# Windowed attention with a gated FFN: tap sums of the second block on TensorE, half swaps by ScalarE copies

## The chip, the cores and the metric

One core of a Trainium2 chip runs the whole program. The metric is the device time of one execution in microseconds (us). TensorE does matrix products, VectorE and ScalarE work elementwise, SyncE issues all DMAs from one queue, and GpSimd does little here.

## The reference

`x` is (4, 4096, 192), `weight_gen` (4, 4096, 8 heads, 7 taps), all fp32.

```python
w = exp(weight_gen - max(weight_gen, -1)); w = w / (sum(w, -1) + 1e-9)   # softmax over 7 taps
out = einsum('bshk,bskhg->bshg', w, x_unf)   # x_unf: tokens s-6 .. s, 8 heads of 24 channels
gate = 1 / (1 + exp(-(out @ w_gate)))        # 192 -> 1536
return (gate * (out @ w_val)) @ w_out        # 1536 -> 192
```

## The kernel before

Channels lie on the partitions and tokens along the free axis. The 16384 tokens are cut into 32 blocks of 512, and the 1536 hidden channels into 12 chunks of 128. A unit is one block with one chunk; there are 384, and `period(s)` gives TensorE the 28 matmuls of one: for unit s the gate and value products (18 matmuls), and for unit s − 2 the output products (10). Two 64-row matmuls run as a pair in the two halves of the array. To keep fp32 accuracy every operand is split in a high and a low part, and each product takes three matmuls (high × high, high × low, low × high).

The inputs of a block are `A` (channels 0 to 127, high and low), `As` (the same with its two 64-partition halves exchanged) and `T` (the last 64 channels, the tokens' two halves first side by side on the two partition halves, and then each also on the other half). `attention` (L700) makes them. `window` (L611) multiplies the seven taps by the softmax weights (L622) and adds them up (L636) on VectorE: seven multiplies and six adds of 128 x 512 for `A` (tiles `x`, `wb`), and as many of 128 x 256 for `T` (tiles `xt`, `wt`). The first block has its own version, `window0` (L663), which takes the weights from PSUM where TensorE spread them (L575), with multiplies L675 and adds L695. Then ScalarE casts the high part (L713 for `A`, L754 for `T`), VectorE subtracts to get the low part (L716, L757), and the halves are exchanged: from the second block on by DMAs through `swap` (L655), for the first block by ScalarE copies (L730 and L733 for `As`, L773 and L776 for `T`).

After the products of a unit ScalarE takes `sg` = sigmoid(gate) (L894), VectorE `h` = value × `sg` (L897), ScalarE the high part `hh` (L900), VectorE the low part `hl` (L903). TensorE uses them two periods later. When a block is done, `evac` (L937) takes the sums out of PSUM (L943, L946, L949) and stores them (L954, L957).

Ten softmaxes cover the tokens, the first small, those from the fourth on 2048 tokens: load of `w` from `weight_gen` (L445; two buffers, w_67 and w_68), maximum (L456), subtraction (L463), exp on ScalarE (L473), sum (L482), reciprocal and product (L495), and a store of the weights `ws`, which `load_wb` (L599) reads back for each block, spread over the partitions. Exp and sigmoid need different tables, so an exp among sigmoids stands between two `ACT_TABLE_LOAD`. During the first block `convert` prepares the twelve chunks of the weights (`W`): load of `raw` (L351), casts and bit work (L361 to L398), six matmuls with the identity `eye` (L406 to L408) that add up the low parts, and casts of the result into `W` (L412).

The order on every engine is made by class `Plan` before the program is written: a list scheduler that walks through all operations with a cost for each, a due time derived from when TensorE needs the result, and buffers that come free. For DMAs it reckons with one shared rate, `BANDWIDTH` in bytes per us, and after time `EARLY` (60 us) adds `MARGIN` (2.5 us) to each landing:

```python
dma_free = max(dma_free, t + dur + self.DMA_START) + o.nbytes / self.BANDWIDTH
o.end = dma_free + self.DMA_END + (self.MARGIN if t > self.EARLY else 0.0)
```

PSUM has eight banks: four for gate and value products (`gv`), two for output sums of the first 128 channels (`ph`), two for the last 64 (`pt`).

Of the kernel before, what the change touches and what calls it, by code (L numbers as in the profile page):

```python
# [9 lines left out]
F32 = mybir.dt.float32  # L10
# [5 lines left out]
ALU = mybir.AluOpType  # L16
# [5 lines left out]
INF = 1e18  # L22
# [14 lines left out]
class Plan:  # L37
# [7 lines left out]
    LAT = {"pe": 0.22, "act": 0.15, "dve": 0.15, "pool": 0.17, "sp": 0.0}  # L45
    SAME = {"pe": 0.0, "act": 0.05, "dve": 0.13, "pool": 0.1, "sp": 0.0}
    WINDOW = 0.15
    BANDWIDTH = 215e3
    DMA_START, DMA_END = 0.6, 1.0
    MARGIN, EARLY = 2.5, 60.0  # L50
    AHEAD = 1.5
# [7 lines left out]
    def place(self, name, bufs):  # L59
        self.places[name] = [dict(buf=b, key=None) for b in bufs]  # L60

    def op(self, engs, fn, deps=(), alloc=(), uses=(), due=INF, table=None, nbytes=0, late=0.0, after=(), lag=None, port=True):

        o = Op(
            len(self.ops), engs, fn, [d for d in deps if d is not None], list(alloc),
            [k for _, k in alloc] + list(uses), due, table, nbytes, late,
            [d for d in after if d is not None], lag, port and ("dve" in engs or "pool" in engs),
        )  # L70
        for d in o.deps + o.after:
            d.succ.append(o)
        for k in o.uses:
            self.key_uses.setdefault(k, []).append(o)
        self.ops.append(o)
        return o
# [19 lines left out]
    def order(self):  # L96
# [69 lines left out]
        while todo:  # L166
            best, tops = None, {}
            for e, lst in ready.items():
                c = [(earliest(o, e), o) for o in lst]
                c = [(t, o) for t, o in c if t is not None]  # L170
                if not c:
                    continue
                t0 = min(t for t, _ in c)
                t, o = min(
                    ((t, o) for t, o in c if t <= t0 + self.WINDOW),
                    key=lambda x: (x[1].due, x[1].seq),
                )
                tops[e] = (t, o, e)
                if best is None or t < best[0]:
                    best = (t, o, e)  # L180
            if "dve" in tops and "pool" in tops and best[2] in ("dve", "pool"):
                d, p = tops["dve"], tops["pool"]
                if d[1].port and p[1].port and abs(d[0] - p[0]) <= self.WINDOW:
                    best = min(d, p, key=lambda x: (x[1].due, x[1].seq))
            assert best, [o.fn for l in ready.values() for o in l]
            t, o, e = best
            for (_, k), b in zip(o.alloc, slots(o)[1] if o.alloc else ()):
                b["key"] = k
                key_buf[k] = b["buf"]
            dur = o.engs[e]  # L190
            if o.table and o.table != table:
                dur += self.TABLE
                table = o.table
            o.eng, o.start = e, t
            if o.port:
                port[e] = t + dur
            free[e] = t + dur
            if e == "sp":
                dma_free = max(dma_free, t + dur + self.DMA_START) + o.nbytes / self.BANDWIDTH
                o.end = dma_free + self.DMA_END + (self.MARGIN if t > self.EARLY else 0.0)  # L200
            else:
                o.end = t + dur
            o.bufs = {k: key_buf[k] for k in o.uses}
            for x in o.engs:
                ready[x].remove(o)
            order.append(o)
            todo -= 1
            for s in o.succ:
                left[s.seq] -= 1
                if not left[s.seq]:  # L210
                    enlist(s)
# [5 lines left out]
def conv_gated_ffn(ctx: ExitStack, tc: tile.TileContext, xt, wg, wcat, outT):  # L217
# [12 lines left out]
    nc = tc.nc  # L230
# [51 lines left out]
    def act(n, psum=False):  # L282
        return (0.05 if psum else 0.093) + 0.000835 * n
# [13 lines left out]
    def op(engs, fn, deps=(), **kw):  # L297

        return plan.op(engs, fn, deps, **kw)

    def both(n):
        return {"dve": dve(n)}
# [133 lines left out]
    def softmax(b, t0, T, base, due=INF):  # L436
# [7 lines left out]
            src = bass.AP(wg.tensor, wg.offset + base, [[K * L, Q], [L, K], [1, L]])  # L444
            nc.sync.dma_start(out=buf[key][:Q, :, :L], in_=src)  # L445

        o_ld = op({"sp": SP}, ld, alloc=[("w", key)], nbytes=P * K * L * 4, due=due)
        step = 64 if L % 64 == 0 else L
        cuts = [(a, min(a + step, L)) for a in range(0, L, step)]
        subs = []  # L450
# [197 lines left out]
        acc_last[0] = m_op[K - 1]  # L648
        return ACC, last

    def swap(key_in, key_out, src, dst, rows, to, fn_deps):


        def f(buf, e):
            nc.sync.dma_start(  # L655
                out=buf[key_out].bitcast(F32)[to, :, dst], in_=buf[key_in].bitcast(F32)[rows, :, src]
            )

        return op({"sp": SP}, f, fn_deps, uses=list({key_in, key_out}), nbytes=R * 2 * M2 * 4)

    LOW, UP = slice(0, R), slice(R, P)

    def window0(parts, cols, X, prods):  # L663

        ACC = ("acc", prods, 0)
        prod = [ACC] + [("prod", prods, k) for k in range(1, K)]
        ms, chain = [[] for _ in range(K)], []
        for i, (t0, first, o_sp, keys_) in enumerate(parts):
            for k in range(K):

                def f_mult(buf, e, t0=t0, first=first, k=k):
                    def four(ap):
                        return ap.rearrange("p (b t) -> p b t", b=4)

                    nc.vector.tensor_tensor(  # L675
                        out=four(buf[prod[k]][:, t0 : t0 + M2]),
                        in0=four(buf[X][:, t0 + k : t0 + k + M2]),
                        in1=bank[:, first : first + 4, k * CH : (k + 1) * CH], op=ALU.mult,
                    )

                ms[k].append(
                    op(
                        {"dve": dve(M2)}, f_mult, x_op[X] + [o_sp] ,
                        port=False, alloc=[] if i else [("prod" if k else "acc", prod[k])],
                        uses=[X] + keys_ + ([prod[k]] if i else []),
                        after=[chain[-1]] if chain else [],
                    )
                )
                chain.append(ms[k][-1])
        last = ms[0]  # L690
        for k in range(1, K):

            def f_add(buf, e, k=k):
                a = buf[ACC][:, :cols]
                nc.vector.tensor_tensor(out=a, in0=a, in1=buf[prod[k]][:, :cols], op=ALU.add)  # L695

            last = [op({"dve": dve(cols)}, f_add, last + ms[k], uses=[ACC, prod[k]])]
        return ACC, last[0]

    def attention(n):  # L700

        A, As = ("A", n), ("As", n)
        if n == 0:
            o_w = soft[0]["st"][0]
            ga = spread("wa", 0, range(4), sel_h, [o_w])
            gb = spread("wc", 4, range(4, 8), sel_h, [o_w])
            ACC, last = window0([(0, 0, *ga), (M2, 4, *gb)], N, ("x", 0), "h")
        else:
            wb = [load_wb(("wb", n), n, i, GH, 0, i) for i in range(2)]
            ACC, last = window(("h", n), N, ("x", n), ("wb", n), wb)  # L710

        def f_hi(buf, e, ACC=ACC):
            nc.scalar.copy(buf[A][:, 0, :], buf[ACC])  # L713
# [8 lines left out]
        lo = op(both(N), f_lo, [hi], uses=[A, ACC])  # L722
        done = []
        for rows, to in ((LOW, UP), (UP, LOW)):
            if n:
                done.append(swap(A, As, slice(0, N), slice(0, N), rows, to, [lo]))
            else:

                def f_shi(buf, e, rows=rows, to=to, ACC=ACC):
                    nc.scalar.copy(buf[As][to, 0, :], buf[ACC][rows, :])  # L730

                def f_slo(buf, e, rows=rows, to=to):
                    nc.scalar.copy(buf[As][to, 1, :], buf[A][rows, 1, :].bitcast(F32))  # L733

                done.append(op({"act": act(N)}, f_shi, [last], uses=[As, ACC], after=[hi]))
                done.append(op({"act": act(N)}, f_slo, [lo], uses=[A, As]))

        ready[n, 0], ready[n, 1] = [hi, lo], done

# [2 lines left out]
        T = ("T", n)  # L742
        if n == 0:
            gt = spread("wd", 0, range(4), sel_t, [o_w])
            ACT_, lastt = window0([(0, 0, *gt)], M2, ("xt", 0), "t")
        else:
            wt = [load_wb(("wt", n), n, i, GT, i * R, 0) for i in range(2)]
            ACT_, lastt = window(("t", n), M2, ("xt", n), ("wt", n), wt)
        his, los = [], []
        for i, rows in enumerate((LOW, UP)):  # L750
            own = slice(i * M2, (i + 1) * M2)
# [12 lines left out]
                   uses=[ACT_] + ([T] if i else []), after=his[-1:])  # L764
            )
            los.append(op(both(M2), f_tlo, [his[-1]], uses=[T, ACT_]))
            if n:
                done.append(swap(T, T, own, own, rows, UP if i == 0 else LOW, [los[-1]]))
            else:
                to = UP if i == 0 else LOW  # L770

                def f_shi(buf, e, rows=rows, to=to, own=own):
                    nc.scalar.copy(buf[T][to, 0, own], buf[ACT_][rows, :M2])  # L773

                def f_slo(buf, e, rows=rows, to=to, own=own):
                    nc.scalar.copy(buf[T][to, 1, own], buf[T][rows, 1, own].bitcast(F32))  # L776

                done.append(op({"act": act(M2)}, f_shi, [lastt], uses=[T, ACT_], after=[his[-1]]))
                done.append(op({"act": act(M2)}, f_slo, [los[-1]], uses=[T]))
        ready[n, 2] = done + his + los  # L780


# [261 lines left out]
```

## Time and profile before

| | us |
|---|---|
| median of 3 runs (lowest, highest) | 1316.96 (1316.7, 1317.54) |
| the profiled execution | 1317.17 |
| its span | 1315.4 |
| TensorE matmul busy | 1273.6 |
| VectorE busy | 1040.1 |
| ScalarE busy | 605.8 |
| bytes moved by DMA | 151.30 MB |

The span is what the profiler recorded from the first to the last instruction; the device time holds 1.8 us more. Busy time counts instructions of the engine alone. The granted clock is the share of full speed that TensorE was given, 1.00 for 2.4 GHz and 0.50 for 1.2 GHz, as a mean over a stretch.

### The profile page before, as it was taken

How to read it: one execution, taken by the hardware profiler on the slowest of the kernel's cores; microseconds unless marked ns; L12 is line 12 of the kernel's file. 1: busy time of each engine (PE TensorE's matmuls, PEld its weight loads, DVE VectorE, ACT ScalarE, POOL GpSimd, SP SyncE). 2: the span in 40 equal slices, each digit the busy share in tenths (PEclk: the TensorE clock that was granted, in tenths of full speed). 3: DMA queues.
4: the chain of work that ended last, by engine and by line, in shares of the span. 5: the costliest groups of instructions: out<-in, count | busy, mean ns of one | idle time of the engine just before them, and what ended most of it. 6: DMA issues, size and time to landing. Idle time of an engine off the chain costs nothing.

```text
span 1315.4 us, 29736 instructions
## 1 busy us (share of the span) xinstructions
PE 1273.6 (97%) x10860; PEld 1071.0 (81%) x10860; DVE 1040.1 (79%) x1904; ACT 605.8 (46%) x1016; POOL 133.8 (10%) x1477
## 2 busy tenths in 40 slices
PE   5989999899999999999999999999999999999998
PEld 3667888678788888888888888888888888888886
DVE  9898989799988887777788777778887777886443
ACT  4744544354544444444444444444444444444443
POOL 0000111001011111111111111111111111111110
PEclk7989999989899999999999999999999999999999
DMA  4578498846545544444554344445534444211100
GB/s 124 164 189 166 115 174 177 211 120 165 139 113 133 133 97 104 115 116 109 126 133 114 93 117 113 117 114 133 123 97 110 111 118 109 69 37 38 37 13 14
DMA packets 57826, 151.30 MB, mean 115 GB/s; under 512 B 10832, under 2 KB 29136, under 8 KB 57680
## 3 DMA queue, kind: packets, MB, share of 16 engines
q1 hardware_dynamic: 57680, 149.40, 47.2%
q8 instruction: 86, 1.41, 0.5%
q14 instruction: 60, 0.49, 0.1%
HBM read 108.86 MB, written 16.14 MB: 95 GB/s over the span
## 4 chain that ended last, share of the span: by engine, by line
PE 78%; DVE 14%; DMA 3%; issue 2%; ACT 2%; SPq 0%; POOL 0%; DVEq 0%; POOLq 0%; ACTq 0%
PE bank L839 77%; DVE acc L636 2%; DVE h L897 2%; DVE hl L903 2%; DVE prod L622 2%; DMA w<-in_weight_gen 2%; DMA wt<-ws 1%; DVE m L482 1%; DMA wb<-ws 1%; DVE m L456 1%; PE bank L406 0%; DVE prod L675 0%; DVE acc L695 0%; DVE acc L622 0%; DVE m L491 0%
## 5 line engine op out<-in xcount | busy, mean ns | idle before, releaser
L839 PE MATMUL bank<-hh,W 64*128 64x512 f32 x2304 | 773.4, 389 | 1.4 <-POOL seen L837 0.7
L839 PE MATMUL bank<-As,W 64*128 64x512 f32 x2304 | 653.5, 390 | 0.0
L839 PE MATMUL bank<-T,W 64*128 64x512 f32 x2304 | 648.1, 389 | 0.0
L839 PE MATMUL bank<-hl,W 64*128 64x512 f32 x1536 | 596.8, 389 | 6.2 <-DVE hl L903 5.9
L839 PE MATMUL bank<-A,W 64*128 64x512 f32 x2304 | 479.1, 390 | 11.5 <-DVE h L897 9.8
L900 ACT CAST hh<-h 128x512 fp32r<-128x512 f32 x384 | 238.6, 622 | 537.0 <-DVE h L897 535.7
L839 PEld LDWEIGHTS bank<-hh,W 64*128 64x128 f32 x2304 | 425.9, 185 | 41.7 <-POOL seen L837 2.5
L839 PEld LDWEIGHTS bank<-T,W 64*128 64x128 f32 x2304 | 426.6, 186 | 38.5
L839 PEld LDWEIGHTS bank<-As,W 64*128 64x128 f32 x2304 | 425.6, 186 | 38.7
L897 DVE TENSOR_TENSOR h<-bank,sg 128x512 f32<-128x512 f32 x384 | 262.6, 684 | 162.8 <-PE bank L839 161.5
L839 PEld LDWEIGHTS bank<-A,W 64*128 64x128 f32 x2304 | 291.8, 186 | 52.4 <-DVE h L897 11.2
L903 DVE TENSOR_TENSOR hl<-h,hh 128x512 fp32r<-128x512 f32 x384 | 263.0, 685 | 87.2 <-ACT hh L900 83.4
L839 PEld LDWEIGHTS bank<-hl,W 64*128 64x128 f32 x1536 | 284.2, 185 | 35.7 <-DVE hl L903 10.5
L894 ACT ACTIVATE sg<-bank 128x512 f32<-128x512 f32 x384 | 230.4, 601 | 119.7 <-PE bank L839 115.7
L837 POOL MEMSET seen<- 1x1 f32 x1471 | 133.0, 90 | 1175.6 <-PE bank L839 1175.2
L636 DVE TENSOR_TENSOR acc<-acc,prod 128x512 f32<-128x512 f32 (+1 forms) x372 | 202.0, 547 | 0.9
L622 DVE TENSOR_TENSOR prod<-x,wb 128x512 f32<-128x512 f32 x186 | 121.7, 678 | 0.1
L622 DVE TENSOR_TENSOR prod<-xt,wt 128x256 f32<-128x256 f32 x186 | 76.9, 414 | 0.0
L757 DVE TENSOR_TENSOR T<-acc,T 64x256 fp32r<-64x256 f32 x64 | 26.6, 416 | 1.0
L754 ACT CAST T<-acc 64x256 fp32r<-64x256 f32 x64 | 25.8, 403 | 2.5 <-DVE acc L695 1.7
L946 ACT COPY ev<-bank 64x512 f32<-64x512 f32 x32 | 18.8, 586 | 16.2 <-PE bank L839 16.1
L406 PE MATMUL bank<-ce,eye 128*128 128x512 f32 (+1 forms) x48 | 19.9, 501 | 5.0 <-DVE prod L675 3.6
(54 smaller groups left out, 346.2 us busy)
## 6 DMA issues: line engine op xcount, KB each, us to landing
wb<-ws SPq DMA_DIRECT2D x62, 896.0 KB
wt<-ws SPq DMA_DIRECT2D x62, 448.0 KB
As<-A SPq DMA_DIRECT2D x62, 256.0 KB
x<-in_x SPq DMA_DIRECT2D x32, 259.0 KB
out<-osb SPq DMA_DIRECT2D x32, 256.0 KB
T<-T SPq DMA_DIRECT2D x62, 128.0 KB
raw<-in_w SPq DMA_DIRECT2D x12, 576.0 KB
xt<-in_x SPq DMA_DIRECT2D x64, 65.5 KB
```

Source lines behind the costliest of these rows:

```text
L406: nc.tensor.matmul(dst, eye[:, 0].bitcast(F32), buf[E].bitcast(F32)[:, a:z], start=True, stop=False)
L622: nc.vector.tensor_tensor(out=buf[prod(k)][:, :cols].rearrange("p (i t) -> p i t", t=M2), in0=buf[X][:, k : k + cols].rearrange("p (i t) - ...
L636: ENG[e].tensor_tensor(out=a, in0=a, in1=buf[prod(k)][:, :cols], op=ALU.add)
L754: nc.scalar.copy(buf[T][rows, 0, own], buf[ACT_][rows, :M2])
L757: ENG[e].tensor_tensor(out=buf[T][rows, 1, own], in0=buf[ACT_][rows, :M2], in1=buf[T][rows, 0, own].bitcast(F32), op=ALU.subtract,)
L837: turn = nc.gpsimd.memset(seen, 0.0)
L839: ins = nc.tensor.matmul(buf[dst], w, m, start=start, stop=stop)
L894: nc.scalar.activation(out=buf[k["sg"]], in_=buf[k["g"]], func=AF.Sigmoid)
L897: nc.vector.tensor_tensor(out=buf[k["h"]], in0=buf[k["v"]], in1=buf[k["sg"]], op=ALU.mult)
L900: nc.scalar.copy(buf[k["hh"]], buf[k["h"]])
L903: ENG[e].tensor_tensor(out=buf[k["hl"]], in0=buf[k["h"]], in1=buf[k["hh"]].bitcast(F32), op=ALU.subtract)
L946: nc.scalar.copy(buf[EV][LOW, :], buf[PT][UP, :])
```

## The change

Three things. First, `window_pe` and `sum_pe` are new: in the second block the seven products of each tap sum go one after another through TensorE, as plain fp32 matmuls with the identity, and add up in a `ph` bank (512 columns) or a `pt` bank (256 columns); VectorE does the multiplies only. The first block's last 64 channels are summed in the same way (`window0` with `where="pt"`). Second, `swap` is gone: the ScalarE copies that only the first block had are used for all blocks. Third, the planner reckons with 190e3 in place of 215e3 bytes per us, and with 12 us more for the landing of a `weight_gen` load.

```diff
-    BANDWIDTH = 215e3
+    BANDWIDTH = 190e3
...
-                o.end = dma_free + self.DMA_END + (self.MARGIN if t > self.EARLY else 0.0)
+                o.end = dma_free + self.DMA_END + (self.MARGIN + o.more if t > self.EARLY else 0.0)
...
-        o_ld = op({"sp": SP}, ld, alloc=[("w", key)], nbytes=P * K * L * 4, due=due)
+        o_ld = op({"sp": SP}, ld, alloc=[("w", key)], nbytes=P * K * L * 4, due=due, more=12.0)
...
+    def window_pe(key, cols, X, W_, wb, where):
+
+        ACC, last, chain = (where, ("sum", key)), None, acc_last[0]
+        for k in range(K):
+            PR = ("prod", key, k)
...
+            chain = op(
+                both(cols), f_mult, x_op[X] + wb, after=[chain], alloc=[("prod", PR)],
+                uses=[X, W_],
+            )
+            last = sum_pe(ACC, PR, cols, k, [last, chain], where)
...
+    def sum_pe(ACC, PR, cols, k, deps, where):
         def f(buf, e):
-            nc.sync.dma_start(
-                out=buf[key_out].bitcast(F32)[to, :, dst], in_=buf[key_in].bitcast(F32)[rows, :, src]
-            )
+            nc.tensor.matmul(
+                buf[ACC][:, :cols], eye[:, 0].bitcast(F32), buf[PR][:, :cols], start=k == 0,
+                stop=k == K - 1,
+            )
...
+        if where:
+            ACC, last = (where, ("sum", prods)), None
+            for k in range(K):
+                last = sum_pe(ACC, prod[k], cols, k, [last] + ms[k], where)
+            return ACC, last
...
-            ACC, last = window(("h", n), N, ("x", n), ("wb", n), wb)
+            args = (("h", n), N, ("x", n), ("wb", n), wb)
+            ACC, last = window_pe(*args, "ph") if n == 1 else window(*args)
...
-            if n:
-                done.append(swap(A, As, slice(0, N), slice(0, N), rows, to, [lo]))
-            else:
...
+            def f_shi(buf, e, rows=rows, to=to, ACC=ACC):
+                nc.scalar.copy(buf[As][to, 0, :], buf[ACC][rows, :])
+
+            def f_slo(buf, e, rows=rows, to=to):
+                nc.scalar.copy(buf[As][to, 1, :], buf[A][rows, 1, :].bitcast(F32))
...
-            ACT_, lastt = window0([(0, 0, *gt)], M2, ("xt", 0), "t")
+            ACT_, lastt = window0([(0, 0, *gt)], M2, ("xt", 0), "t", "pt")
...
-            ACT_, lastt = window(("t", n), M2, ("xt", n), ("wt", n), wt)
+            args = (("t", n), M2, ("xt", n), ("wt", n), wt)
+            ACT_, lastt = window_pe(*args, "pt") if n == 1 else window(*args)
...
-            if n:
-                done.append(swap(T, T, own, own, rows, UP if i == 0 else LOW, [los[-1]]))
-            else:
-                to = UP if i == 0 else LOW
```

Since the planner's costs and operations differ, the order moves on all engines. A line number of the changed kernel is up to 30 higher for the same operation. Three places follow.

ScalarE at the end of the first block, where the second block's `A_85` and `T_89` are made and the last chunk of the weights (`W_125`) is converted. Before:

```order
L398 CAST W_125<-ce_109 128x576
L900 CAST hh_96<-h_92 128x512
L412 CAST W_125<-bank 128x512
L412 CAST W_125<-bank 128x64
L713 CAST A_85<-acc_83 128x512
L754 CAST T_89<-acc_81 64x256 x2
L900 CAST hh_94<-h_93 128x512
```

Now:

```order
L926 CAST hh_95<-h_92 128x512
L744 CAST A_85<-bank 128x512
L758 CAST As_87<-bank 64x512
L783 CAST T_89<-bank 64x256 x2
L761 CAST As_87<-A_85 64x512
L758 CAST As_87<-bank 64x512
L761 CAST As_87<-A_85 64x512
L799 CAST T_89<-bank 64x256
L802 CAST T_89<-T_89 64x256
L799 CAST T_89<-bank 64x256
L802 CAST T_89<-T_89 64x256
L413 CAST W_125<-bank 128x512
```

The casts of `A_85` and `T_89` and eight copies, which read PSUM or the tile itself, now stand ahead of the casts of `W_125`.

SyncE's queue at the loads of softmaxes 6 and 7 (`w_68`, `w_67`). Before:

```order
L445 DMA w_68<-in_weight_gen 128x896
L655 DMA As_87<-A_85 64x1024 x2
L655 DMA T_89<-T_89 64x2x256 x2
L599 DMA wb_72<-ws_132 128x1x1792
L954 DMA out<-osb_102 128x512
L957 DMA out<-osb_103 64x512
L327 DMA x_63<-in_x 128x518
L599 DMA wb_72<-ws_132 128x1x1792
L327 DMA xt_65<-in_x 64x262
L599 DMA wt_74<-ws_132 64x1x1792
L327 DMA xt_65<-in_x 64x262
L599 DMA wt_74<-ws_132 64x1x1792
```

Now:

```order
L600 DMA wt_73<-ws_131 64x1x1792
L446 DMA w_68<-in_weight_gen 128x896
L446 DMA w_67<-in_weight_gen 128x896
L600 DMA wb_72<-ws_132 128x1x1792
L328 DMA x_63<-in_x 128x518
L600 DMA wb_72<-ws_132 128x1x1792
```

Before, the load of `w_67` came right after the twelve rows shown; now it stands behind that of `w_68`, with no transfers between.

ScalarE around the exps of softmaxes 4 and 5 (`w_68`, `w_67`). Before, the exp of the fourth stands at period 12 and that of the fifth at period 28, and each looks like this:

```order
L894 ACTIVATE sg_91<-bank 128x512
L473 ACT_TABLE_LOAD
L473 ACTIVATE w_68<-w_68 128x896
L900 CAST hh_96<-h_93 128x512
L894 ACT_TABLE_LOAD
L894 ACTIVATE sg_90<-bank 128x512
```

Now, at periods 27 and 28:

```order
L920 ACTIVATE sg_90<-bank 128x512
L799 CAST T_89<-acc_82 64x256
L802 CAST T_89<-T_89 64x256
L474 ACT_TABLE_LOAD
L474 ACTIVATE w_68<-w_68 128x896
L926 CAST hh_96<-h_92 128x512
L920 ACT_TABLE_LOAD
L920 ACTIVATE sg_91<-bank 128x512
L474 ACT_TABLE_LOAD
L474 ACTIVATE w_67<-w_67 128x896
L926 CAST hh_94<-h_93 128x512
L920 ACT_TABLE_LOAD
```

The two exps follow each other with one sigmoid between. Counted by sigmoids, the later exps stood at periods 59, 61, 80, 82 and 92 and now stand at 69, 71, 81, 82 and 93.

## Rows read from the trace of the kernel before

**Rows 1.** The page, busy time, share of the span and instructions of each engine.

```profile
PE 1273.6 (97%) x10860; PEld 1071.0 (81%) x10860; DVE 1040.1 (79%) x1904; ACT 605.8 (46%) x1016; POOL 133.8 (10%) x1477
```

**Rows 2.** Windows: stretch, length, busy of PE, PEld, DVE, ACT, POOL, PEclk, DMA share, GB/s.

```profile
0.00:27.57 27.57, 12.09 (x28) 7.47 (x29) 24.65 (x57) 10.30 (x16) 0.71 (x6) 0.82 0.43 123
75.36:119.54 44.18, 36.51 (x242) 27.90 (x240) 40.01 (x79) 18.64 (x31) 2.68 (x30) 0.85 0.80 172
154.45:164.67 10.22, 10.17 (x87) 7.74 (x85) 9.39 (x18) 7.34 (x10) 1.08 (x12) 1.00 0.85 194
256.70:275.85 19.15, 10.41 (x60) 7.45 (x57) 11.19 (x22) 8.59 (x12) 0.67 (x7) 0.64 0.63 148
336.14:351.81 15.67, 13.58 (x87) 9.69 (x85) 14.20 (x27) 10.81 (x14) 1.07 (x12) 0.78 0.27 68
380.37:389.08 8.71, 7.68 (x58) 5.46 (x56) 6.58 (x13) 6.00 (x8) 0.71 (x8) 1.00 0.09 18
391.00:1306.00 915.00, 915.00 (x8078) 783.13 (x8076) 682.85 (x1229) 408.56 (x694) 98.85 (x1105) 1.00 0.40 98
```

**Rows 3.** Waits: who waited for what, us in total, times, longest.

```profile
PE bank L839 <- DVE h L897: 9.8, 4, 7.5
...
DVE m L456 <- DMA w<-in_weight_gen: 8.6, 1, 8.6
```

**Rows 4.** SyncE's timeline at 224 to 246, and the chain's piece for that load.

```profile
224.75 4.29 SPq L655 DMA_DIRECT2D As<-A  x2
...
245.90 0.44 SPq L445 DMA_DIRECT2D w<-in_weight_gen  x1
...
245.90 17.01 DMA w<-in_weight_gen
```

**Rows 5.** ScalarE's timeline from 335.7: start, us, engine, line, operation.

```profile
335.71 1.28 ACT L473 ACT_TABLE_LOAD   x1
337.01 0.95 ACT L473 ACTIVATE w<-w 128x896 f32<-128x896 f32 x1
337.98 1.28 ACT L894 ACT_TABLE_LOAD   x1
```

**Rows 6.** Groups of lines: count, busy us, mean ns, idle before.

```profile
L900 ACT CAST hh<-h 128x512 fp32r<-128x512 f32 x384 | 238.6, 622 | 537.0 <-DVE h L897 535.7
...
L894 ACT ACTIVATE sg<-bank 128x512 f32<-128x512 f32 x384 | 230.4, 601 | 119.7 <-PE bank L839 115.7
...
L636 DVE TENSOR_TENSOR acc<-acc,prod 128x512 f32<-128x512 f32 x186 | 126.7, 681 | 0.9
...
L412 ACT CAST W<-bank 128x512 fp32r<-128x512 f32 x12 | 7.0, 582 | 3.4 <-PE bank L408 3.4
...
L695 DVE TENSOR_TENSOR acc<-acc,prod 128x256 f32<-128x256 f32 x6 | 2.5, 417 | 0.0
...
L730 ACT CAST As<-acc 64x512 fp32r<-64x512 f32 x2 | 1.2, 616 | 0.0
...
L773 ACT CAST T<-acc 64x256 fp32r<-64x256 f32 x2 | 0.8, 403 | 0.0
```

**Rows 7.** TensorE's timeline, one conversion among main matmuls: start, us.

```profile
66.89 1.13 PE L406 MATMUL bank<-ce,eye 128*128 128x512 f32 x2
...
68.08 0.39 PE L408 MATMUL bank<-cr,eye 128*128 128x512 f32 x1
68.30 0.33 PE L406 MATMUL bank<-ce,eye 128*128 128x64 f32 x2
...
68.76 0.50 PE L839 MATMUL bank<-hh,W 64*128 64x512 f32 x1
```

**Rows 8.** VectorE's and TensorE's timelines at a block's edge.

```profile
743.60 0.68 DVE L903 TENSOR_TENSOR hl<-h,hh 128x512 fp32r<-128x512 f32 x1
...
745.64 0.39 PE L839 MATMUL bank<-hl,W 64*128 64x512 f32 x1
```

## What the change was predicted to do

> **What bounds the kernel now.** I read the page's busy shares first. TensorE is busy 97% of the span and no other engine over 81% [rows 1]: it is the bound, and a change earns only where TensorE stands still or runs at half its clock. So the second view is the same shares cut into stretches. In the last stretch, 391 to 1306, TensorE is busy for all 915.00 us at a granted clock of 1.00 [rows 2]. Its 8078 matmuls there give 0.1133 us each, so a period (one unit of work, 28 matmuls) lasts 3.172 us; the reader is to see that 70% of the span has nothing to lose. What is lost lies ahead of 391, and each other row of that group is one place: length less its whole periods.
>
> - 75.36 to 119.54, where the second block is prepared: 8 periods (25.38) and two weight conversions of 1.87 (68.76 less 66.89, [rows 7]) leave 15.1 us lost. Idle time (44.18 − 36.51 = 7.7) and clock (15% of 44.18 = 6.6) come to nearly the same.
> - 154.45 to 164.67, 3 periods with one exp of the softmax: 10.22 − 9.52 = 0.7.
> - 256.70 to 275.85, 2 periods: 19.15 − 6.34 = 12.8, the largest single stall.
> - 336.14 to 351.81, 3 periods with two exps: 15.67 − 9.52 = 6.15, at a clock of 0.78.
> - 380.37 to 389.08, 2 periods: 8.71 − 6.34 = 2.4.
>
> The third view, the waits, says whose stall the 12.8 is: TensorE waited once 7.5 us for VectorE's h, and VectorE once 8.6 us for a load of weight_gen [rows 3]. The fourth, SyncE's queue and the chain, says why: the load was issued at 245.90 and landed 17.01 later, and the queue had stood 4.29 us at the swap As<-A before it [rows 4].
>
> The profiled execution took 1317.17 us, 1.8 outside the span, and is 0.2 above the median of the runs; I sum against 1317.17. About 0.2%, 2.6 us, is what a measurement of this kernel can tell from no change.
>
> **The start.** The first block's last 64 channels are summed on TensorE. Removed: 6 adds of 0.417 = 2.5 us of VectorE [rows 6]. Added: 7 plain fp32 matmuls of 256 columns. No row has one, but a conversion does: from 66.89 to 68.30 go one fp32 matmul of 512 columns and two others at 0.22 (68.08 to 68.30), so the fp32 one is 1.41 − 0.44 = 0.97 [rows 7], and 256 columns about 0.48. The clock in the first 27.57 us averages 0.82 [rows 2], so the seven take 3.4 to 4 us. Five stand ahead of the first conversion, beside multiplies that come at VectorE's pace; the last two stand behind it, next to the first main matmul. At half clock these two are 1.9 us on the path, less a little of VectorE's gain: I take **+1.5**. Ends: −2.5 (the adds go, the sums are hidden) and +3.5 (all seven in line).
>
> **The second block.** Added: 7 × 0.97 + 7 × 0.48 = 10.2 us of TensorE, in the middle of the main matmuls, where nothing hides them, for it is the bound. Removed: 6 × 0.681 [rows 6] and as many at about 0.41, 6.6 us of VectorE. ScalarE gets, ahead of the casts of the last conversion, a chain that the order shows: one A cast and four As copies (0.616 each), two T casts and four T copies (0.403), 5.5 us, and then W's own 0.582 [rows 6]. TensorE has only two sums and a conversion, 2.8 us, before it needs W: 3.3 us of standing still. In the old stretch each idle us cost 0.86 more at the lower clock (6.6 to 7.7, [rows 2]), here 2.8. Together 16.3 instead of the 15.1 lost now, which VectorE's and the swaps' lateness and the exp of the fourth softmax (moved on to period 27) caused: **+1.2**. Ends: −4.9 (ScalarE's chain fits into its gaps and only the 10.2 of the sums stay) and +4 (2.8 of the old idle time stays as well, as VectorE still does the fourteen multiplies).
>
> **The copies instead of swaps.** Two As and two T transfers of each block from the second on leave SyncE's queue, and what they cost the two loads behind them is counted below. On ScalarE come, for each block, 4 × 0.616 + 4 × 0.403 = 4.1 us [rows 6] per 12 periods, 38.1 us. ScalarE is busy 408.56 of 915.00 there [rows 2], 17.0 of 38.1; it becomes 21.1, still 55%. What waits in its queue is the cast hh behind a copy. At a block's edge now, hl is ready at 743.60 + 0.68 and TensorE first takes such a tile at 745.64 [rows 8]: 1.3 us in hand, and one copy in front costs at most 0.62. I cost it at **0**. The cover is that 1.3 us; without it, see the second rival.
>
> **The moved loads.** In the planner's reckoning with 12 us more allowed for the landing, both loads of softmaxes 6 and 7 stand together in SyncE's queue, ahead of the block's other loads and with no swap before them; they are used some 20 periods later (about 60 us) instead of 17.01 us [rows 4] later. The 12.8 goes. What is late next is not a load but ScalarE: two exps each, now at periods 69 and 71.
>
> Each exp costs ScalarE two table loads of 1.28 and 0.95 of its own [rows 5], with sg 0.60 and hh 0.62 a period of 4.73 against 3.17 ([rows 6] for these two). One exp alone lost 0.7 the third of [rows 2]; two of them two periods apart lost 6.15. By the new order:
>
> - softmaxes 4 and 5 at periods 27 and 28, one apart: the excess over two periods is 2 × 1.56 = 3.1, and I take 3.5, a little for the clock, where one alone lost 0.7: **+2.8** (0.7 to 6.15).
> - 6 and 7 at 69 and 71, the pattern that lost 6.15 at 336: −12.8 + 6.15 = **−6.65**.
> - 8 and 9 at 81 and 82, one apart: 3.5 for the 6.15 of now: **−2.65** (0.7 to 6.15 again).
> - 10, at 93 instead of 92: 2.4 as now, 0.
>
> The Trainium skill (ScalarE: Activation LUTs, section What ACT_TABLE_LOAD costs) gives a switch as 1283 ns and another 1380 ns of drain. The trace has the 1283 ns and the next exp 0.02 us behind it (335.71 + 1.28 to 337.01, [rows 5]), so no drain is seen. By the page two exps would take 5.5 us more.
>
> **Sum:** 1.5 + 1.2 + 0 + 2.8 − 6.65 − 2.65 = −3.8, and 1317.17 − 3.8 = **1313.4**.
>
> **Rivals.**
>
> *Pairs cost what the pair at 336 costs.* The switches are a queue on ScalarE, and the clock falls to half while TensorE waits (0.78 there, [rows 2]). If each of the three pairs loses 6.15, the terms are 1.5 + 1.2 + 5.45 − 6.65 + 0 = +1.5: 1318.7, no change. For it: the only pair measured. Against it: in that pair VectorE's rows for two softmaxes also fell together.
>
> *ScalarE makes hh late at each block's edge (slower).* If the planner's copies stand not one but in twos and threes ahead of hh, the 1.3 us are used up: three are 1.85 (0.55 too late), two 1.23 (in time). It decides from a delay of 1.3 us on. At a mean of 0.3 us over 31 blocks it adds 9.3: 1322.7. For it: eight copies must go somewhere in the three periods of an edge, where ev and osb also come. Against it: a queue at 55%, and a planner that sees it.
>
> *The exps cost only 0.7 each* (as the one at 154, [rows 2]) and the start comes free: 0 + 1.2 + 0.7 − (12.8 − 1.4) − (6.15 − 1.4) = −14.2: 1302.9. For it: VectorE has lost its waits for loads. Against it: the 336 pair.
>
> **Chances.** The forecast's mechanism 0.49, its own range 1309 to 1318 by the ends above; pairs dear 0.18; ScalarE late at the edges 0.18; exps cheap 0.15. Faster by over 0.2% (below 1314.3): two thirds of the forecast's and all of the cheap case, 0.48. Within: a third of the forecast's and two thirds of the dear pairs, 0.28. Slower (above 1319.6): 0.24. The range 1303 to 1321 leaves out half of the cheap case and some two thirds of the slower one, 0.2.
>
> **What would show it.** Right: no wait of VectorE for weight_gen over 1 us; seven fp32 matmuls of 0.9 to 1.0 us and seven of half that near 100 us; TensorE waiting 2 to 4 us for W's cast there; losses of 3 to 6 us around periods 28, 70 and 82; no idle TensorE after 391. Wrong: a load of weight_gen still late; TensorE waits on hl or hh once a block; the sums at twice 0.97 us; a stretch around the second block of over 50 us.

## The result: slower by 0.9%

The changed kernel takes 1328.28 us (median of 4 runs, 1326.95 to 1329.54) against 1317.25 for the kernel before (4 runs beside them); the ratio is 1.0092, 95% interval 1.007 to 1.0113. Forecast were 1313.4 and a range up to 1321. The profiled execution took 1329.43 us, its span is 1327.6, so 12.2 us of span have to be found.

The page of the changed kernel, busy time and share of each engine (the answer to [rows 1]):

```profile
PE 1291.6 (97%) x10902; PEld 1046.9 (79%) x10902; DVE 1037.8 (78%) x1886; ACT 708.4 (53%) x1264; POOL 133.9 (10%) x1477
```

ScalarE has 102.6 us more, VectorE 2.3 less. TensorE is still the bound. So again the stretches, the changed kernel's windows with the columns of [rows 2]:

```profile
0.00:28.46 28.46, 13.11 (x36) 9.25 (x36) 24.36 (x54) 9.01 (x14) 0.71 (x6) 1.00 0.45 127
76.82:120.99 44.17, 41.49 (x270) 31.63 (x268) 33.18 (x62) 19.36 (x36) 2.94 (x30) 0.96 0.80 168
152.73:166.65 13.92, 11.79 (x87) 8.83 (x85) 13.92 (x26) 12.02 (x17) 1.11 (x12) 0.88 0.21 61
256.70:275.85 19.15, 19.15 (x168) 15.19 (x166) 18.34 (x35) 12.65 (x24) 1.97 (x22) 1.00 0.78 167
296.60:309.08 12.48, 10.04 (x60) 6.80 (x57) 12.48 (x25) 9.27 (x12) 0.71 (x8) 0.75 0.30 72
338.00:354.91 16.91, 13.83 (x116) 10.45 (x114) 16.88 (x32) 12.60 (x17) 1.43 (x16) 1.00 0.51 125
384.20:395.07 10.87, 9.28 (x59) 6.35 (x57) 7.04 (x14) 7.43 (x11) 0.72 (x8) 0.84 0.29 70
399.00:1314.00 915.00, 914.83 (x8004) 747.73 (x8002) 679.53 (x1221) 477.39 (x869) 97.93 (x1095) 1.00 0.32 78
```

The fourth row is the stretch of the old 12.8 us stall: TensorE is now busy in it throughout. The last row is where nobody could lose anything: TensorE reads as busy and at full clock, but did 8004 matmuls in 915.00 us where it had done 8078 in [rows 2]. 74 matmuls at 0.1133 us are 8.4 us. They are lost in pieces too short to show as idle time.

Where each microsecond went is read best from the sigmoids, one per period, numbered from 0. This table has the start of a few (us in the trace), and the difference to the kernel before:

| sigmoid | before | changed | difference | what lies ahead of it |
|---|---|---|---|---|
| 4 | 51.11 | 52.57 | +1.47 | the start |
| 16 | 118.66 | 120.12 | +1.45 | the second block |
| 35 | 179.66 | 184.83 | +5.17 | softmaxes 4 and 5 |
| 55 | 243.13 | 249.90 | +6.77 | two block edges |
| 66 | 290.84 | 285.82 | −5.02 | the old 12.8 us stall |
| 78 | 328.92 | 330.97 | +2.05 | softmaxes 6 and 7, now here |
| 87 | 363.63 | 364.45 | +0.82 | softmaxes 8 and 9 |
| 98 | 400.91 | 404.92 | +4.01 | softmax 10 |
| 383 | 1305.31 | 1316.42 | +11.11 | the rest, 24 blocks |

Step by step, forecast and measured: start +1.5 and +1.5; second block +1.2 and 0.0; softmaxes 4 and 5 +2.8 and +3.7; the old stall together with 6 and 7 −6.65 and −4.7 (2.05 less 6.77); 8 and 9 −2.65 and −1.2; 10, 0 and +3.2; the rest, 0 and +7.1; the edges between 35 and 55, 0 and +1.6. Some of the difference at 55 to 98 is also block edges. The last 1.1 of the 12.2 us lie behind the last sigmoid and were not followed.

### The profile page after: what moved, and what is told of

It reads as the page before. It is cut to its first block, busy times and chain, and to the rows that moved or that the text cites. A ratio compares the mean times of both kernels' runs of the same rounds, so it can differ in the third digit from the quotient of the medians.

```text
span 1327.6 us, 29745 instructions
## 1 busy us (share of the span) xinstructions
PE 1291.6 (97%) x10902; PEld 1046.9 (79%) x10902; DVE 1037.8 (78%) x1886; ACT 708.4 (53%) x1264; POOL 133.9 (10%) x1477
## 4 chain that ended last, share of the span: by engine, by line
PE 86%; DVE 8%; ACT 3%; issue 1%; DMA 0%; POOL 0%; ACTq 0%; DVEq 0%; POOLq 0%
PE bank L865 83%; DVE h L923 1%; DVE acc L637 1%; DVE hl L929 1%; DVE prod L623 1%; PE bank L677 1%; PE bank L407 1%; DVE m L457 1%; ACT sg L920 0%; DMA out<-osb 0%; ACT As L761 0%; DVE w L464 0%; ACT As L758 0%; ACT hh L926 0%; DVE prod L700 0%
## 5 line engine op out<-in xcount | busy, mean ns | idle before, releaser
L865 PE MATMUL bank<-A,W 64*128 64x512 f32 x2304 | 473.6, 388 | 3.3 <-DVE h L923 1.8
L865 PEld LDWEIGHTS bank<-A,W 64*128 64x128 f32 x2304 | 287.1, 185 | 50.4 <-DVE h L923 2.6
L637 DVE TENSOR_TENSOR acc<-acc,prod 128x512 f32<-128x512 f32 (+1 forms) x360 | 197.8, 551 | 0.4
L623 DVE TENSOR_TENSOR prod<-xt,wt 128x256 f32<-128x256 f32 x180 | 72.9, 418 | 0.0
L761 ACT CAST As<-A 64x512 fp32r<-64x512 f32 x64 | 39.5, 617 | 0.9
L758 ACT CAST As<-acc 64x512 fp32r<-64x512 f32 x62 | 38.4, 619 | 1.1
L975 DVE TENSOR_TENSOR osb<-bank,ev 64x512 f32<-64x512 f32 x32 | 21.8, 682 | 18.6 <-ACT ev L972 18.6
```

Of the source, the lines that this page charges most:

```text
L623: nc.vector.tensor_tensor(out=buf[prod(k)][:, :cols].rearrange("p (i t) -> p i t", t=M2), in0=buf[X][:, k : k + cols].rearrange("p (i t) - ...
L637: ENG[e].tensor_tensor(out=a, in0=a, in1=buf[prod(k)][:, :cols], op=ALU.add)
L865: ins = nc.tensor.matmul(buf[dst], w, m, start=start, stop=stop)
L975: nc.vector.tensor_tensor(out=buf[OT][LOW, :], in0=buf[PT][LOW, :], in1=buf[EV][LOW, :], op=ALU.add)
```

## What is new in the traces

**The late stretch.** The waits of the changed kernel from 480 to 1290 (who waited for whom: us in all, times, longest):

```profile
DVE osb L975 <- ACT ev L972: 12.2, 21, 1.1
PEld bank L865 <- DVE hl L929: 12.2, 40, 0.5
DVE acc L623 <- ACT As L758: 9.2, 19, 0.5
```

None of the three stands in the same answer for the kernel before. The stretch has 21 blocks: about once in each VectorE waits half a microsecond for the tile acc and once more than half for ev, and twice the weight loads of TensorE wait for hl. One edge shows it. ScalarE's timeline of the changed kernel (start, length):

```profile
474.30 0.62 ACT L758 CAST As<-acc 64x512 fp32r<-64x512 f32 x1
474.95 0.60 ACT L920 ACTIVATE sg<-bank 128x512 f32<-128x512 f32 x1
475.57 0.62 ACT L761 CAST As<-A 64x512 fp32r<-64x512 f32 x1
476.20 0.62 ACT L758 CAST As<-acc 64x512 fp32r<-64x512 f32 x1
476.73 0.61 ACT L761 CAST As<-A 64x512 fp32r<-64x512 f32 x1
477.37 0.62 ACT L926 CAST hh<-h 128x512 fp32r<-128x512 f32 x1
...
479.69 0.40 ACT L802 CAST T<-T 64x256 fp32r<-64x256 f32 x1
480.00 0.58 ACT L969 COPY osb<-bank 128x512 f32<-128x512 f32 x1
480.60 0.58 ACT L972 COPY ev<-bank 64x512 f32<-64x512 f32 x1
```

and VectorE's, with what it waited for in brackets:

```profile
475.68 0.69 DVE L923 TENSOR_TENSOR h<-bank,sg 128x512 f32<-128x512 f32 x1 [0.50 <-PE bank L865]
476.86 0.43 DVE L623 TENSOR_TENSOR acc<-xt,wt 128x256 f32<-128x256 f32 x1 [0.48 <-ACT As L758]
...
481.22 0.68 DVE L975 TENSOR_TENSOR osb<-bank,ev 64x512 f32<-64x512 f32 x1 [0.56 <-ACT ev L972]
...
491.70 0.68 DVE L929 TENSOR_TENSOR hl<-h,hh 128x512 fp32r<-128x512 f32 x1
```

ScalarE runs without a break from 473.88 (a T cast) to 482.4. From here two paths lead to TensorE, one to each of the two weight loads that wait in a block.

The first path is ScalarE's own queue, at the block's second unit. In the kernel before, the cast hh of that unit started 0.03 us after its h:

```profile
742.07 0.68 DVE L897 TENSOR_TENSOR h<-bank,sg 128x512 f32<-128x512 f32 x1
742.78 0.62 ACT L900 CAST hh<-h 128x512 fp32r<-128x512 f32 x1
```

In the changed kernel h ends at 480.32 and hh starts 0.89 us later, behind two T copies, osb and ev; hl follows hh at once, and the weight load waits for it:

```profile
479.64 0.68 DVE L923 TENSOR_TENSOR h<-bank,sg 128x512 f32<-128x512 f32 x1
481.21 0.62 ACT L926 CAST hh<-h 128x512 fp32r<-128x512 f32 x1
481.86 0.69 DVE L929 TENSOR_TENSOR hl<-h,hh 128x512 fp32r<-128x512 f32 x1
482.61 0.18 PEld L865 LDWEIGHTS bank<-hl,W 64*128 64x128 f32 x1 [0.20 <-DVE hl L929]
```

The second path leads over VectorE. The As copy at 476.20 reads acc, so the next block's first tap product cannot be written before it ends; ev comes behind the T copies. VectorE stands 1.0 us for ScalarE in these two places, and 0.50 ahead of h where it has nothing else to do while acc is held. Then comes its own full stretch, the tap sums of the next block, where it is busy nearly back to back until 499. It cannot catch up, and the order of its rows is fixed. Some 15 us after the copies, hl ends at 492.38, and TensorE's matmul:

```profile
492.02 0.39 PE L865 MATMUL bank<-As,W 64*128 64x512 f32 x1
492.44 0.49 PE L865 MATMUL bank<-hl,W 64*128 64x512 f32 x1
```

starts 0.42 us after its neighbour, where 0.22 is usual. The reader is to see that on this path cause and loss are four to five periods apart. Of the 12.2 us that weight loads waited for hl, 4.1 belong to the first path (the block's second unit, 21 waits) and 8.0 to the second (its fifth unit, 19 waits). In TensorE's own time the first costs about 0.1 us a block and the second about 0.3 (from one unit's first hl matmul to the next unit's, means of 20 blocks).

**The second block.** TensorE's timeline in the changed kernel (x4 is two sums, each recorded as two):

```profile
84.28 0.73 PE L865 MATMUL bank<-A,W 64*128 64x512 f32 x4
84.94 1.98 PE L677 MATMUL bank<-prod,eye 128*128 128x512 f32 x4
86.85 0.50 PE L865 MATMUL bank<-A,W 64*128 64x512 f32 x1
...
88.66 2.42 PE L677 MATMUL bank<-prod,eye 128*128 128x512 f32 x8
91.01 0.50 PE L865 MATMUL bank<-hh,W 64*128 64x512 f32 x1
...
98.46 2.08 PE L407 MATMUL bank<-ce,eye 128*128 128x512 f32 x2 [2.37 <-ACT As L758]
```

Two sums of 512 columns take 1.91 (84.94 to 86.85), 0.96 each; one of 512 and three of 256 take 2.35, so 0.46 each: the forecast's 0.97 and 0.48. The Trainium skill (FP8 and Floating Point Precision, section TensorE Precision Notes) counts four passes for true fp32. The trace agrees: 0.96 is a little over four times the 0.22 of the split form in [rows 7]. The one long stop is that of the last conversion, for an As copy: it needs the PSUM bank that the copy still reads.

**The exps.** The pair of softmaxes 4 and 5, ScalarE's timeline of the changed kernel:

```profile
155.21 1.28 ACT L474 ACT_TABLE_LOAD   x1
156.51 0.95 ACT L474 ACTIVATE w<-w 128x896 f32<-128x896 f32 x1
157.36 0.60 ACT L926 CAST hh<-h 128x512 fp32r<-128x512 f32 x1
157.98 1.28 ACT L920 ACT_TABLE_LOAD   x1
```

The exp starts 0.02 us after its table load, as before; no other cost of the switch shows. The 13.92 us of that window are 3 periods and 4.4 us, where 3.5 was taken.

## Experiments

The common measure is the time from sigmoid 107 to 383, 23 blocks: 875.84 us in the kernel before, 883.73 in the changed one, 0.34 more per block. The kernel before, run 21 times beside some of these, spread from 1310.56 to 1319.19 us around its median of 1316.28, so a microsecond or two between medians says little; the times from sigmoid to sigmoid are each of one execution.

**Swaps back.** From the third block on `swap` instead of the copies:

```diff
         for rows, to in ((LOW, UP), (UP, LOW)):
+            if n > 1:
+                done.append(swap(A, As, slice(0, N), slice(0, N), rows, to, [lo]))
+                continue
...
+            if n > 1:
+                done.append(swap(T, T, own, own, rows, to, [los[-1]]))
+                continue
```

> Undoes one part of the change: from the third block on the halves are exchanged by DMAs again; the sums on TensorE, the second block's copies and the planner's numbers stay. Theory A (the ScalarE copies cost the 0.3 to 0.4 us per block that the changed kernel loses after 391, 7.1 us in all from sigmoid 98 to 383): that stretch comes back to 904.4 us, as before, and the time falls by 7 or more, to 1318 to 1322. Theory B (the sums and the moved softmaxes cost it, the late loss has another cause such as the planner's numbers): the late loss stays, 1327 to 1330.

Measured: 1314.82 us (1312.92 to 1316.4), ratio to before 0.9987 [0.9976, 0.9997]; from 107 to 383 875.83, no loss. Theory A holds: the copies are the late loss. The time fell even further than expected, by 13.5 us. The two profiled executions lie 16.5 apart; 9.4 of this is there by sigmoid 98, where edges and the moved order of the softmaxes are not told apart.

**Copies that read A and T.** The copies of the high parts now wait for the casts of A and T and no longer hold acc.

```diff
-                nc.scalar.copy(buf[As][to, 0, :], buf[ACC][rows, :])
+                nc.scalar.copy(buf[As][to, 0, :], buf[A][rows, 0, :].bitcast(F32))
...
-                nc.scalar.copy(buf[T][to, 0, own], buf[ACT_][rows, :M2])
+                nc.scalar.copy(buf[T][to, 0, own], buf[T][rows, 0, own].bitcast(F32))
```

> The changed kernel with one edit: the copies of the high parts read the tiles A and T in place of the tap sum acc, so that acc is free when A's low part is made and VectorE need not wait 0.5 us per block for As copies before the next block's first multiply. Theory A1 (that wait for acc is what makes VectorE late and with it hl): the late stretch loses under 0.1 us per block, time 1320 to 1323. Theory A2 (the burst of eight copies at the block's edge on ScalarE is the cause, whatever it reads: ev and the next casts queue behind it): still 0.3 to 0.4 us per block, 1326 to 1330.

Measured: 1318.84 us (1316.51 to 1319.69), ratio 1.0022 [1.0013, 1.0032]; from 107 to 383 881.33, 0.24 per block. Neither theory as stated: a third of the late loss went together with the wait for acc, two thirds stayed. Between the two profiled executions lie 10.5 us, 8.1 of them ahead of 107, where the order also moved. The waits of this kernel from 480 to 1290 no longer have acc, but ev and hl are still there (in a block's second unit and now in its sixth):

```profile
DVE osb L975 <- ACT ev L972: 11.6, 20, 1.1
PEld bank L865 <- DVE hl L929: 9.4, 39, 0.3
```

**Copies read A and T, and held back.** With the edit above, the copies of a block wait for the sigmoid of chunk 6 of the block before:

```diff
+        if f == 6 and n and n + 1 < NB:
+            for c in copies[n + 1]:
+                c.after.append(o)
+                o.succ.append(c)
```

> The copies read A and T, as in the run before, and those of a block are held back until the sixth period of the block before it, away from the edge where ScalarE also does the casts of A and T and empties PSUM. Both theories of the copies (acc held, burst at the edge) expect no loss per block: the late stretch 904 to 905 us, time 1317 to 1322. If the late stretch still loses 0.3 per block, neither is the cause and the sheer sum of ScalarE's work would be.

Measured: 1314.93 us (1312.96 to 1316.18), ratio 0.9986 [0.9973, 1.0]; from 107 to 383 875.84. From sigmoid 98 on it is 906.8, above the expected 904 to 905, for the last exp now stands at period 104. The time is below the expected range. Behind 107 the sum of ScalarE's work costs nothing; its place does.

**Held back to behind ev only.** The same with `f == 2`:

> As the run with delayed copies, but held back only until the second period of the block before, so that ev, osb and the casts of A and T go first and the eight copies follow in one burst in the middle of VectorE's tap sums. If the loss per block comes from ev and the casts queued behind the copies at the edge (VectorE idles there and cannot catch up): no loss per block from sigmoid 107 to 383 (875.84 us as before). If any burst ahead of hh makes VectorE late while it is full: 0.2 us or more per block, 880 or more there.

Measured: 1313.77 us (1312.76 to 1317.5), ratio 0.9991 [0.9976, 1.0006]; from 107 to 383 875.84. The eight copies come in one burst, in the middle of VectorE's full stretch, and cost nothing. Its edge, ScalarE's timeline:

```profile
470.35 0.58 ACT L979 COPY ev<-bank 64x512 f32<-64x512 f32 x1 [0.47 <-PE bank L868]
```

and VectorE's:

```profile
467.00 0.42 DVE L623 TENSOR_TENSOR acc<-xt,wt 128x256 f32<-128x256 f32 x1
...
471.49 0.67 DVE L982 TENSOR_TENSOR osb<-bank,ev 64x512 f32<-64x512 f32 x1
```

Now ScalarE waits for TensorE's sum and not VectorE for ScalarE: the tap sums begin at once and the fold (osb) has no wait. This kernel, too, copies from A and T, so against the 0.24 us per block of the run that does so at the edge the place is what differs. What hurts is that ev, hh and the casts stand behind the copies there. Early this variant is slower (sigmoid 9 is 17.0 us behind the kernel before, sigmoid 16 then 4.6), in another order of the conversions and softmaxes; that was not followed up.

**T by DMA, As by ScalarE.** The changed kernel with `swap` for T alone from the third block on.

> The changed kernel with the T tiles exchanged by DMAs from the third block on and only the four As copies on ScalarE (2.5 instead of 4.1 us per block). If the loss per block grows with ScalarE's burst: a third to a half of the changed kernel's 7.9 us from sigmoid 107 to 383 stays, 3 to 5 us. If the wait of VectorE for acc, which As copies alone cause, is most of it: 6 us or more stays. If only the queue in front of ev counts and four copies fit: under 1 us.

Measured: 1311.67 us (1309.78 to 1312.5), ratio 0.9969 [0.9953, 0.9984]; from 107 to 383 875.87. Four copies fit. The wait for ev came once in this kernel, 0.3 us. A wait for acc is not in its list, although the As copies still read acc: reading it is not by itself what costs.

**Copies alone.** The kernel before with `if n:` made `if False:` at the two swaps, so that all blocks copy.

> The kernel before with the ScalarE copies for all blocks alone: no sums on TensorE beyond the first block's, planner's numbers as before. Theory A (copies cost 0.3 to 0.4 per block): the late stretch 911 to 912 us; without the swaps on SyncE's queue the 12.8 us stall at 257 to 276 goes, and the pairs of exps cost 3 to 6 each; 1315 to 1325. Theory B (late loss from the sums or the planner's numbers): late stretch 904.4, 1305 to 1315.

Measured: 1331.63 us (1329.38 to 1332.9), ratio 1.0115 [1.0093, 1.0138]; from 107 to 383 889.38, 0.59 per block, more than was expected, and the time is above both ranges. Theory A holds against B, but the size differs from kernel to kernel: in this one TensorE's weight loads waited for hl 19.4 us in 59 places from 480 to 1290, three a block. Why it is three here and two in the changed kernel stays open; the waits for acc and ev are as many, and the changed kernel without the sums (below) has three as well. Two more things: the 12.8 us stall is gone without the planner's numbers (between sigmoids 55 and 66 this kernel gains 10.7), and sigmoid 16 comes 5.3 us earlier than before, with the tap sums still on VectorE.

**Planner's numbers alone.**

```diff
-    BANDWIDTH = 215e3
+    BANDWIDTH = 190e3
...
-        o_ld = op({"sp": SP}, ld, alloc=[("w", key)], nbytes=P * K * L * 4, due=due)
+        o_ld = op({"sp": SP}, ld, alloc=[("w", key)], nbytes=P * K * L * 4, due=due, more=12.0)
```

> The kernel before with the planner's two numbers alone (190e3 bytes per us, 12 us more for weight_gen loads); swaps stay DMAs, no new sums. The exps stand at periods 24, 28, 68, 80, 82, 92 and 94. If the moved loads are what takes the 12.8 us stall at 257 to 276 away: no wait over 1 us for weight_gen, the loss there under 1 us, late stretch 904.4 as before, 1305 to 1311. If the swaps on SyncE's queue are what made the load late: a wait of 4 us or more stays, 1313 to 1318.

Measured: 1312.09 us (1310.33 to 1314.79), ratio 0.9969 [0.9953, 0.9984]; no wait for weight_gen; the old stall's window is full:

```profile
256.70:275.85 19.15, 19.15 (x172) 15.67 (x168) 18.40 (x37) 9.30 (x17) 1.95 (x22) 1.00 0.99 192
```

The time is 1 us above the first range and below the second. The stall goes with the swaps still in the queue, but not because the loads are earlier: those of softmaxes 6 and 7 were issued at 223.83 and 245.90 before and are issued at 241.65 and 280.05 here. Their use moved, for the planner now reckons with a later landing, and the exps stand at 286 and 326 us instead of 255 and 272. In the kernel before, VectorE came to the second load's data 8.5 us after its issue and waited the 8.6 of [rows 3]; here it comes to the first load's 16.9 us after the issue and waits for nothing:

```profile
241.65 0.33 SPq L446 DMA_DIRECT2D w<-in_weight_gen  x1
258.53 1.82 DVE L457 TENSOR_REDUCE m<-w 128x64 f32<-128x448 f32 x2
```

**No sums in the second block.** The changed kernel with `window` in place of `window_pe`.

> The changed kernel without the sums of the second block on TensorE (VectorE adds them again); the first block's t sums, the copies and the planner's numbers stay. If the 10 us of fp32 matmuls are paid on the path: the stretch from sigmoid 4 to 16 is 5 us or more shorter than the changed kernel's 67.55, time 1321 to 1325. If VectorE, relieved of 6.6 us, gives them back: that stretch is no shorter, 1326 to 1331.

Measured: 1324.2 us (1324.05 to 1325.57), ratio 1.0058 [1.0037, 1.0079]. From sigmoid 4 to 16 it takes 61.28 us, the changed kernel 67.55: the sums cost 6.3 us there (4.9 counted from the start, for this kernel comes to sigmoid 4 1.3 us later). The late loss of this kernel is larger, 13.1 us from 107 to 383, which takes part of that back.

**Copies in the second block alone, and the planner's numbers.** `if n:` becomes `if n > 1:` at the swaps of the kernel before; no new sums.

> The kernel before with the ScalarE copies in the second block alone, DMAs from the third on, the planner's two numbers, and no new sums. If the sums cost and copies in one block are free: start as before (0), sigmoid 16 some 5 us earlier than before, late stretch 904.4, time 1302 to 1309. If the sums on TensorE helped: not below the run with swaps back (1314.8).

Measured: 1305.23 us (1302.63 to 1305.33), ratio 0.9906 [0.9884, 0.9929]: the fastest, 11.9 us under the kernel before. Start as before, sigmoid 16 5.1 us earlier, no loss from 107 to 383.

**Held-back copies in all blocks, and the planner's numbers, no sums.**

> The kernel before with the copies for all blocks, read from A and T and held back to the sixth period, and the planner's two numbers; no new sums. If DMA swaps cost nothing late and the copies nothing when held back, this stands within 2 us of the run with copies in the second block alone, 1303 to 1311; if ScalarE's 4.1 us per block cost something anywhere, 3 us or more above it.

Measured: 1308.53 us (1308.05 to 1310.7), ratio 0.9939 [0.9918, 0.9961]; 3.3 above the run before (2.7 in the traces, all of it ahead of sigmoid 107). That just meets the second expectation, but the two intervals overlap, so whether the copies cost anything early stays open; which early place it would be was not tried.

**The margin alone.** The fastest kernel with 215e3 bytes per us again.

> The run with copies in the second block alone, with the planner's rate back at 215e3 bytes per us, so that only the 12 us for weight_gen loads is left. If that margin is what moves the loads: the stretch at 257 to 276 stays free and the time is within 3 us of 1305. If the lower rate does it: a wait for weight_gen comes back and the time is 1310 or more.

Measured: 1308.78 us (1307.67 to 1310.09), ratio 0.9953 [0.9937, 0.9969]. No wait for weight_gen comes back, so the 12 us do it, though the time is 3.6 us above the run with both numbers where 3 was allowed. In the traces the two lie 2.3 apart; up to sigmoid 16 the run here is 1.2 ahead, and by 35 it is 2.0 behind, where the exps of softmaxes 4 and 5 stand at periods 27 and 29 instead of 28 and 29. That this order is what the lower rate is worth was not tested.

## Why the prediction was wrong

**Right.** The bound, the old stall and its cause (between sigmoids 55 and 66 the changed kernel gains 11.8 of the 12.8). The price of the sums on TensorE (0.96 and 0.46 for 0.97 and 0.48). The second block's balance, +1.2 forecast and 0.0 measured, came from two terms that cancel. The run without the sums shows them as 6.3 us, and the kernel before with the copies alone gains 5.3 in the same place. The idle time that was put down to W's casts behind ScalarE's chain was there with 2.4 of the 3.3 us, but at the conversion ahead of them, which waited for the PSUM bank that an As copy reads.

**Right by luck.** The start's +1.5 came out, but its reason did not: the two last sums were to run at half clock, 1.9 us, and the granted clock of the first 28.46 us is 1.00, where it had been 0.82. They took 1.04:

```profile
27.41 1.11 PE L677 MATMUL bank<-prod,eye 128*128 128x256 f32 x4
28.45 0.96 PE L865 MATMUL bank<-A,W 64*128 64x512 f32 x6
```

The first main matmul comes 0.9 us later than before (28.45 for 27.57); what adds the rest by sigmoid 4 was not followed.

**The step that failed** is the term of the copies, "I cost it at **0**", and within it the cover: "1.3 us in hand, and one copy in front costs at most 0.62". The 1.3 us were read at one unit. Two units on, where VectorE adds up the next block's taps, hl had only 0.94 us in hand in the kernel before:

```profile
750.36 0.68 DVE L903 TENSOR_TENSOR hl<-h,hh 128x512 fp32r<-128x512 f32 x1
...
751.98 0.39 PE L839 MATMUL bank<-hl,W 64*128 64x512 f32 x1
```

And it is not one copy that stands in front. The eight copies come at the edge as a burst, together with the casts of A and T, ev and osb. At the edge shown hh stands 1.0 us behind its h in the block's first unit (476.37 to 477.37) and 0.9 in the second. VectorE waits there for acc and for ev, 1.0 us together, and then has a full stretch. The prediction's own sign of being wrong, "TensorE waits on hl or hh once a block", came about twice a block. Measured are 0.34 us per block, 7.1 from sigmoid 98 on and more ahead of it: with the copies taken off the edge the changed kernel is 13.5 us faster (swaps back) and 13.4 (held back), part of it by an early order that moved with them. That the copies are the cause of the late loss is shown by these two runs, that the place is, by the two held-back ones, which have all the copies and no loss after 107. How the late loss divides between acc and the rest is not shown: a third of it went in the run that reads A, but the order moved there too.

**The rival** "ScalarE makes hh late at each block's edge" had the right sign, the right place and nearly the right size (0.3 a block), with the chance 0.18. Its path, hh late in ScalarE's queue, is there in the block's second unit, with a third of the weight loads' waits (4.1 of 12.2 us); the larger part is an hl that is late through VectorE's waits, which the rival did not have. The reason given against it, a planner that sees it, was no reason: the planner sees the queue, but starts whatever can start first, and the copies can start as soon as A and T are there, a whole block before TensorE needs them.

**Sizes.** The exps of 4 and 5 cost 3.7 more than before where 2.8 was taken. For 8 and 9 and for 10 the forecast was too low by 1.5 and 3.2; how much of this is block edges was not separated. No pair was as cheap as 0.7 per exp. Of the 16.0 us between the forecast's −3.8 and the span's +12.2 the copies' late loss is 7.1, the terms of the softmaxes are 7.5 (0.9, 1.9, 1.5 and 3.2), the edges from 35 to 55 and the end 2.7; the second block gives 1.2 back. How much of the softmaxes' part is the copies, too, was not separated.

## What to carry to other kernels

Work that is given to an engine with time to spare needs a place as well as time: look at what else that engine does at the same edge, and at which buffers the new work holds and who writes them next. Read the time in hand at every unit around the edge, not at one. An engine at 79% can have stretches at 100%, and a wait of half a microsecond just ahead of one can come out at the end of it as the bound engine's loss, periods later and in pieces too small for idle time; count the work done per stretch. Where a change has several parts, time each alone: here the planner's numbers and one block's copies were worth 11.9 us, and the kernel with all three parts was 11 us slower than the one before.

## What was not expected of the hardware

The matmul records count TensorE as busy 914.83 of 915.00 us in a stretch that holds 74 fewer matmuls: a late operand of 0.2 to 0.4 us leaves no idle time in the busy share. The wait shows with the weight loads instead (PEld, 12.2 us in 40 places).
